# A rewritten work order for the first stage of a linear-attention and feed-forward kernel, with thirteen weight slices in place of ten beside the attention

## The chip, the core and the metric

The kernel runs on one core of one Trainium2 chip. A core has a matrix engine (PE, whose weight loads are shown apart as PEld), a vector engine (DVE), a scalar engine (ACT), a general engine (POOL) and a queue engine (SP) that only issues DMAs. Each engine works through its own instructions strictly in the order in which they were written, and waits at semaphores for what the others have to finish. The metric is the device time of one execution in microseconds (us); less is better.

## The reference, cut to what matters

```python
# q, k, v: (8 batches, 8 heads, 576 tokens, 64); omega: (128, 64)
q_s, k_s = q * scale, k * scale
def phi(x):
    proj = einsum('bhsd,md->bhsm', x, omega)
    h = proj - sum(x * x, axis=-1, keepdims=True) / 2
    h = h - max(h, axis=-1, keepdims=True)
    return exp(h) / sqrt(m)
q_p, k_p = phi(q_s), phi(k_s)
kv = einsum('bhsm,bhsd->bhmd', k_p, v)
z = sum(k_p, axis=2)
num = einsum('bhsm,bhmd->bhsd', q_p, kv)
den = einsum('bhsm,bhm->bhs', q_p, z)[..., None] + 1e-6
x = (num / den) as (4608 tokens, 512)
h = x @ w_in                      # (512, 2048), float64 weights
out = (h - tanh(h)) @ w_out       # (2048, 512), float64 weights
```

## The kernel before

**Tiling.** The 4608 tokens are cut into 18 chunks of 256. Eight heads are handled as four pairs (index c, 0 to 3). The 2048 hidden units are cut into 16 slices of 128 (index f, 0 to f in hexadecimal). A slice of the weights holds 128 columns of `w_in` and the matching 128 rows of `w_out`. The weights arrive as float64; the kernel decodes each slice to a high and a low part (two float32r numbers) and multiplies high by high, high by low and low by high.

**The first stage** does everything at once: the attention of batches 0 and 1 (unit `k<b><c>` for the keys, `q<chunk><c>` for the queries of chunks 0 to 2), the decoding of all 16 weight slices (`d<f>`), and the feed-forward of chunks 0 and 1 together (`f<s>`, 512 tokens wide). Its order is written out by hand, or by a program, in the string `ORDER`: each token names a unit, a step of it and, where needed, a buffer slot. `q12.pj.7` is the projection of chunk 1, pair 2, into PSUM bank 7. Lines 678 to 682 of the program walk through the tokens and emit each step's instructions, so the order of the tokens is the order of the instructions on every engine, SP and POOL included. No engine takes work out of this order.

**Steps of a key unit k.** `lk` and `lv` load keys and values (L474, L478, on SP), `pool` copies the last 64 keys and values of each head into the zeroed tiles `kd` and `vd` (L483, L484, four copies on POOL), `pjA`, `pjB`, `pj5` project (L454, L488, PE), `red*` take a row minimum (L460, L492, DVE), `exp*` the exponential (L465, L496, ACT), `pk0` and `pk1` sum keys by values (L500, L510, PE), `z`, `zt`, `zb` spread the key sums, `kvf`, `kvwa`, `kvwd` copy the result out.

**Steps of a query unit q.** `lq` loads (L550, SP), `pj`, `red`, `exp` as above, `den` the denominators (L561, DVE), `nD` and `nA` divide, `pt` transposes (L580, PE), `qt` copies (ACT), `pn` multiplies by the key-value sums (L590, PE), `xh` and `xl` split the result into high and low (L594, L604).

**Steps of a slice d.** `ld` loads 1 MB of float64 words (L618, SP), `b` scales the upper words (L623, ACT), `cl` clamps (L627: POOL, or DVE for slices 0 and 1), `v1`, `v2`, `v3` put the bits together (L630 to L637, DVE), `hi` writes the high part of the weights and `nh` its second copy (L642, L645, ACT), `di` is a DMA that POOL issues and that adds the decoded number to the second copy, so that the low part is left (L648). Only when this DMA has landed can the slice be used in full.

**Steps of a feed-forward unit f.** `h` is 12 matmuls of 512 columns (L380), of which the third already needs the slice's low part; `th`, `g`, `gh`, `gl` form h - tanh(h) and split it (ACT, DVE, ACT, DVE); `o` is 12 more matmuls (L410 to L412). `f0` to `fd` stand in the table; the last two slices follow it in `step`.

**Buffers.** `NW = 10` slices have a place of their own beside the attention's buffers (pool `a0`). The other six take the space of `a0`, which is closed at the token `da.ld`: `if f == NW: close_pool("a0")`, L614. SP therefore waits at these loads for the last users of the attention's buffers. Key, value and query loads rotate through three, three and two buffers.

After the table, the chunks 2 to 17 are processed in a steady loop with the feed-forward of a chunk beside the attention of later ones; there a scheduler, not the table, sets the order.

Of the kernel before, what the change touches and what calls it, by code (L numbers as in the profile page):

```python
# [33 lines left out]
ORDER = """
k03.lk.0 q00.lq.0 k00.lk.1 k02.lk.2 q02.lq.1 k03.lv.0 q00.pj.0 d1.ld q02.pj.1 q00.red k03.pjB.2 k03.pool
q00.exp.0 q02.red k00.pjB.3 k03.redB q02.exp.1 q12.lq.0 k03.pj5.4 k00.redB q03.lq.1 k03.pjA.5 k03.expB.2
k00.lv.1 k03.red5 k00.pjA.6 k03.redA k00.expB.3 k13.lk.0 q12.pj.7 k00.redA k03.expA.4 k02.lv.2 q03.pj.0 q12.red
k00.expA.5 k00.pool q01.lq.0 k03.pk0.3 q10.lq.1 q03.red d3.ld k03.exp5.0 k13.pjB.1 q03.exp.6 k02.pool k03.pk1
k13.redB q12.exp.7 q01.pj.2 k03.z k13.expB.2 k03.zt q01.red k11.lk.1 q10.pj.5 k03.kvf k03.zb d1.b.0 q03.den
k00.pj5.6 k13.lv.0 k00.pk0.4 q01.exp.4 q13.lq.0 k02.pj5.0 q10.red k13.pjA.7 d0.ld q03.nA q03.nD k02.red5  # L40
k02.pjA.1 d3.b.1 k13.redA k13.pool k00.red5 q03.pt.3 k02.redA k00.exp5.1 k02.pjB.2 q10.exp.6 d1.cl d3.cl
k00.pk1 d1.v1 q03.qt.0 k01.lk.0 k02.redB k02.exp5.0 q03.pn.6 k00.kvf k12.lv.1 d1.v2 k02.expB.3 k13.pj5.5
k11.pjA.3 k12.lk.2 k13.red5 k13.expA.5 k00.z d1.v3 k00.zt q20.lq.1 k01.pjB.0 k00.zb d4.ld d0.b.2 q00.den
k13.pk0.4 d1.hi k12.pool k12.pjB.2 q00.nD q10.den q00.nA k01.pjA.7 k13.exp5.1 q03.xh q00.pt.5 d1.nh d9.ld
k11.redA k13.pk1 q03.xl q10.nA q10.nD d1.di k01.redB k12.pj5.6 q00.qt.1 k13.kvwa k12.red5 k01.expB.0 k13.z
q00.pn.5 k01.redA d0.cl k13.zt q00.xh k01.lv.0 q10.pt.0 d0.v1 k13.zb k02.expA.2 q00.xl d6.ld k13.kvwd q20.pj.5
d3.v1 q10.qt.0 d3.v2 k13.kvf k12.exp5.1 q10.pn.1 k01.expA.5 k01.pool k02.pk0.4 q20.red q10.xh d4.b.0 d0.v2
k02.pk1 q11.lq.1 d2.ld q20.exp.6 q10.xl d4.cl k01.pj5.0 k02.z k12.pjA.6 d0.v3 k02.kvf k11.expA.2 k02.zt
k01.pk0.7 k12.redA k02.zb k01.red5 q11.pj.1 k12.expA.3 k12.redB q12.den k11.lv.2 q13.pj.5 k01.exp5.0 d0.hi
q22.lq.1 k01.pk1 q12.nD d7.ld q12.nA q02.den k11.pjB.3 d0.nh k11.pool q02.nD q12.pt.4 q02.nA q11.red q22.pj.6  # L50
k01.kvf k11.redB q12.qt.1 d0.di k11.pj5.0 q11.exp.0 q13.red q12.pn.4 k10.lv.0 k11.red5 q22.red k11.expB.5
q02.pt.1 k10.lk.0 d4.v1 q12.xh k01.z d4.v2 d5.ld q02.qt.0 k01.zt q13.exp.7 q02.pn.3 q12.xl d4.v3 k12.expB.1
k11.pk0.4 k10.pool k10.pjB.1 k01.zb q13.den d4.hi q23.lq.0 k10.pj5.5 k10.pjA.2 q21.lq.1 k11.exp5.0 q01.den
q13.nA d8.ld k11.pk1 q02.xh d2.b.2 q11.den q23.pj.7 k11.kvf k11.kvwa d2.cl q22.exp.2 q11.nD q21.pj.0 q13.nD
q02.xl q11.nA q01.nD q13.pt.6 q01.nA k11.z k11.kvwd q11.pt.3 k10.redA q13.qt.1 k11.zt k10.redB k11.zb q01.pt.6
q11.qt.0 k10.red5 q13.pn.4 q21.red k10.expB.5 q23.red q11.pn.3 q01.qt.1 d2.v1 q13.xh q01.pn.1 k10.expA.7 d2.v2
k12.pk0.6 q01.xh q13.xl q11.xh q01.xl d4.nh k12.pk1 q11.xl d2.v3 q23.exp.0 d4.di k10.pk0.4 k12.z d3.v3 k12.kvwa
k12.zt k12.kvf d2.hi f1.h.7 k12.kvwd q23.den k12.zb d3.hi d2.nh f0.h.6 q22.den f1.th d2.di q23.nA d7.b.0 f1.g
q22.nA q23.nD d7.cl f4.h.7 q22.nD f1.gh d3.nh f1.gl f0.th k10.exp5.0 f0.g q21.exp.4 q22.pt.2 f2.h.6 d6.b.2
q21.den d3.di f0.gh d6.cl q22.qt.0 f0.gl q21.nA q22.pn.1 q21.nD f4.th d7.v1 q23.pt.3 q22.xh f4.g k10.pk1  # L60
q23.qt.1 d7.v2 f0.o k10.kvwa k10.kvf d5.b.1 k10.z k10.kvwd d6.v1 d6.v2 d5.cl d6.v3 f1.o f4.gh f4.gl d6.hi d7.v3
f2.th d6.nh q23.pn.0 f2.g d5.v1 k10.zt f2.gh d6.di q21.pt.7 d5.v2 k10.zb f3.h.6 d7.hi f2.gl q23.xh d7.nh
q20.den q21.qt.0 d7.di f2.o f3.th q20.nD q20.nA f3.g d5.v3 d8.b.2 q20.pt.4 d5.hi d8.cl f6.h.7 q20.qt.1 f3.gh
d9.b.0 f3.gl d5.nh q20.pn.0 q21.pn.6 f6.th d5.di q20.xh d8.v1 f3.o q21.xh f6.g d9.cl da.ld d8.v2 d8.v3 f4.o
f6.gh d8.hi f6.gl db.ld d8.nh d9.v1 d9.v2 f5.h.6 d8.di da.b.1 d9.v3 da.cl dd.ld d9.hi f7.h.7 f5.th d9.nh f5.g
f5.gh dc.ld db.b.2 f5.gl d9.di f8.h.6 da.v1 f7.th db.cl da.v2 da.v3 f5.o de.ld f7.g da.hi da.nh db.v1 f6.o
dc.b.0 da.di db.v2 df.ld f7.gh dc.cl db.v3 f9.h.7 f7.gl db.hi db.nh f8.th db.di dd.b.1 f7.o f8.g dc.v1 f8.gh
dd.cl dc.v2 f8.gl fa.h.6 dc.v3 f9.th f9.g dc.hi f9.gh f8.o dd.v1 df.b.2 f9.gl dd.v2 fa.th df.cl dc.nh fa.g
fb.h.7 dd.v3 fa.gh fa.gl dd.hi dd.nh f9.o dc.di df.v1 fb.th df.v2 dd.di fb.g fa.o df.v3 fb.gh fb.gl df.hi
de.b.0 fc.h.6 df.nh de.cl fd.h.7 fc.th fc.g fc.gh df.di fc.gl fb.o de.v1 fd.th de.v2 fd.g de.v3 fc.o fd.gh  # L70
fd.gl de.hi de.nh fd.o de.di
# [4 lines left out]
def favor_attention_ffn(ctx: ExitStack, tc: tile.TileContext, qT, kT, va, vt, omT, w, out):  # L76
# [74 lines left out]
    nc.gpsimd.tensor_scalar(om_bd[D:P, 1], omf[D:P], -SCALE, 1.0, op0=ALU.mult, op1=ALU.mult)
# [4 lines left out]
    def kv_tiles(pool, names):

        ts = [(pool.tile([P, 9, E], F32, name=f"v{i}"), pool.tile([P, P], F32, name=f"kd{i}"),
               pool.tile([P, 2, E], F32, name=f"vd{i}")) for i in names]
# [4 lines left out]
        return ts

# [303 lines left out]
    def native_k(b, c):  # L469
        u, n = {}, f"k{b}{c}"  # L470

        def lk(slot):
            u["f"] = tile_at("kf", slot, [P, S], F32, f"{n}_f")
            nc.sync.dma_start(u["f"], kT[c, :, b * S : (b + 1) * S])  # L474

        def lv(slot):
            u["v"], u["kd"], u["vd"] = vtiles[slot]
            nc.sync.dma_start(u["v"][:, :, 0:D], va[b, c])  # L478

        def pool():  # L480
            for h in range(2):
                r = slice(h * D, h * D + D)
                nc.gpsimd.tensor_copy(u["kd"][r, r], u["f"][r, 4 * P : S])  # L483
                nc.gpsimd.tensor_copy(u["vd"][r, h], u["v"][r, 4])  # L484

        def pj5(slot):
            u["pj5"] = ps.tile([P, M], F32, tag=BANKS[slot], name=f"{n}_pj5")
            nc.tensor.matmul(u["pj5"], u["kd"], oms, start=True, stop=True)  # L488
# [9 lines left out]
        def pk(h):  # L498
            for t in range(4):
                nc.tensor.matmul(u["pk"][:, E * h : E * h + E], u["ph", 2 * (t // 2)][:, 2 * (t % 2) + h],  # L500
                                 u["v"][:, 5 * h + t], start=(h, t) == (0, 0), stop=False)
# [6 lines left out]
        def pk1():  # L508
            pk(1)
            nc.tensor.matmul(u["pk"][:, 0 : 2 * E], u["ph5"], u["vd"].rearrange("p h e -> p (h e)"),  # L510
                             start=False, stop=True)
# [21 lines left out]
        def zb():  # L533
            zb = att("zb0" if b == 0 else "zb", [P, 2, M], F32, f"{n}_zb")
            nc.scalar.copy(zb.rearrange("p h m -> p (h m)"), u["pk"][:, 256:512])
# [74 lines left out]
    def decoder(f):  # L610
# [9 lines left out]
        def b(slot):  # L620
            u["a"] = dec.tile([P, 2 * DM], U32, tag=f"a{slot}", name=f"a{f}")
            u["af"] = u["a"].bitcast(F32)
            nc.scalar.activation(u["af"], u["raw"].bitcast(F32)[:, 1::2], AF.Copy, scale=2.0**-112)  # L623

        def clamp():
            engine = nc.vector if f < 2 else nc.gpsimd
            engine.tensor_scalar(u["af"], u["af"], -TOP, TOP, op0=ALU.max, op1=ALU.min)  # L627

        def shift():
            nc.vector.tensor_scalar(u["a"], u["a"], 3, None, op0=ALU.logical_shift_left)  # L630

        def low():
# [151 lines left out]
```

## Time and profile before

| | us |
|---|---|
| median of 3 runs | 1075.91 |
| lowest and highest | 1070.32, 1076.04 |
| the profiled execution | 1073.08 |
| its span (first to last instruction) | 1071.3 |

The profiled execution lies 2.8 us under the median, inside the three runs. What lies outside the span is 1.8 us.

PE is busy for 97% of the span, DVE for 78%, ACT for 65%, POOL for 31%. These are averages over a first stage of about 170 us, in which all engines and the DMA queues are loaded, and a steady loop of about 900 us in which PE is hardly ever idle. In 40 slices of the span, the DMA engines' share (in tenths) begins with 8973842111: the first stage loads the attention's inputs and 16 MB of weights. Matmuls are pipelined, so the distance between the starts of two of them says more than the duration of one.

### The profile page before, as it was taken

What the parts mean: (1) busy time and instruction counts of PE and PEld (TensorE: products, weight loads), DVE (VectorE), ACT (ScalarE), POOL (GpSimd) and SP (SyncE); (2) the same over time, 40 slices, a digit from 0 to 9 for tenths busy, and PEclk for the clock granted to TensorE, in tenths of its full rate; (3) what the DMA queues carried; (4) which work ended last, traced back from release to release, by engine and by line L of the source; (5) the groups of instructions that cost most, each with busy time, mean ns of one, the idle gap of its engine ahead of it and who ended that gap; (6) DMA issues with size and microseconds to landing.
All of it is one profiled execution on the core that took longest, in us unless ns stands there. A gap on an engine that the chain in (4) does not pass through costs nothing.

```text
span 1071.3 us, 20143 instructions
## 1 busy us (share of the span) xinstructions
PE 1042.3 (97%) x6760; PEld 948.5 (89%) x6760; DVE 832.1 (78%) x2878; ACT 693.4 (65%) x1773; POOL 333.6 (31%) x569
## 2 busy tenths in 40 slices
...
GB/s 253 291 235 69 260 84 64 52 38 43 33 53 33 54 32 31 11 52 34 52 33 43 43 28 52 32 44 32 52 22 47 34 41 11 31 11 26 1 21 20
DMA packets 37831, 64.27 MB, mean 60 GB/s; under 512 B 12512, under 2 KB 21856, under 8 KB 35680
## 3 DMA queue, kind: packets, MB, share of 16 engines
...
q8 instruction: 53, 0.87, 0.3%
...
## 4 chain that ended last, share of the span: by engine, by line
PE 85%; DVE 6%; DMA 4%; ACT 3%; issue 1%; POOL 1%; SPq 0%; DVEq 0%; ACTq 0%; POOLq 0%
PE h L380 35%; PE po L410 11%; PE po L411 11%; PE po L412 11%; PE pk L243 3%; PE pj_q L184 2%; PE pt L332 2%; PE pn L344 2%; DMA w<-a 1%; PE pn L343 1%; DMA k_f<-kT 1%; PE k_pj L454 1%; PE pj_kb L184 1%; PE pj_ka L184 1%; PE k_pk L500 1%
## 5 line engine op out<-in xcount | busy, mean ns | idle before, releaser
L380 PE MATMUL h<-xh,w 128*128 128x256 f32 (+1 forms) x2176 | 451.3, 291 | 8.6 <-DMA w<-a 5.2
L380 PEld LDWEIGHTS h<-xh,w 128*128 128x128 f32 x2176 | 356.2, 191 | 19.6 <-DMA w<-a 5.9
L380 PE MATMUL h<-xl,w 128*128 128x256 f32 (+1 forms) x1088 | 317.1, 292 | 1.1 <-DVE xl L357 1.1
L380 PEld LDWEIGHTS h<-xl,w 128*128 128x128 f32 x1088 | 208.1, 191 | 7.5 <-DVE xl L357 1.3
L410 PE MATMUL po<-w,gh 128*128 128x512 f32 x544 | 213.9, 393 | 0.2 <-ACT gh L391 0.2
L411 PE MATMUL po<-w,gh 128*128 128x512 f32 x544 | 213.5, 392 | 0.0
L412 PE MATMUL po<-w,gl 128*128 128x512 f32 x544 | 211.5, 391 | 0.0
L391 ACT CAST gh<-g 128x512 fp32r<-128x512 f32 x144 | 89.5, 621 | 100.8 <-DVE g L388 94.4
L388 DVE TENSOR_TENSOR g<-h,g 128x512 f32<-128x512 f32 x144 | 98.8, 686 | 64.6 <-ACT g L386 63.4
L386 ACT ACTIVATE g<-h 128x512 f32<-128x512 f32 x144 | 85.2, 592 | 92.7 <-PE h L380 79.7
L394 DVE TENSOR_TENSOR gl<-g,gh 128x512 fp32r<-128x512 f32 x144 | 111.0, 771 | 41.0 <-ACT gh L391 39.2
L412 PEld LDWEIGHTS po<-w,gl 128*128 128x128 f32 x544 | 102.3, 188 | 20.9
L410 PEld LDWEIGHTS po<-w,gh 128*128 128x128 f32 x544 | 102.5, 188 | 16.7 <-ACT gh L391 0.4
L411 PEld LDWEIGHTS po<-w,gh 128*128 128x128 f32 x544 | 102.5, 188 | 15.3
L192 ACT ACTIVATE phi_q<-phi_q,nb_q 128x128 f32<-128x128 f32 x240 | 79.3, 392 | 5.8 <-DVE nb_q L188 5.5
L322 DVE CUSTOM_DVE_ANT_0 junk<-phi_q,zb 128x128 f32<-128x128 f32 (+1 forms) x240 | 71.8, 299 | 13.2 <-ACT phi_q L192 0.3
L235 POOL CAST vhl<-v 128x128 fp32r<-128x128 f32 (+1 forms) x144 | 46.1, 321 | 87.5 <-PE pk L243 74.5
L227 POOL TENSOR_TENSOR khl<-phi_ka,khl 128x256 fp32r<-128x256 f32 x48 | 37.5, 788 | 110.3 <-DVE khl L226 102.1
L337 DVE TENSOR_TENSOR ql<-pt,qh 128x512 fp32r<-128x512 f32 x60 | 41.1, 685 | 30.2 <-ACT qh L336 30.0
L627 POOL TENSOR_SCALAR a<-a 128x1024 f32<-128x1024 f32 x14 | 54.5, 3892 | 17.4 <-ACT a L623 17.0
L188 DVE CUSTOM_DVE_ANT_0 phi_q<-pj_q,phi_q 128x128 f32<-128x128 f32 x240 | 56.0, 284 | 1.3 <-ACT phi_q L185 1.0
L336 ACT CAST qh<-pt 128x512 fp32r<-128x512 f32 x60 | 34.9, 581 | 32.2 <-PE pt L332 32.0
...
## 6 DMA issues: line engine op xcount, KB each, us to landing
...
qf<-qT SPq DMA_DIRECT2D x60, 128.0 KB, 2.1
...
```

The lines of the kernel that those rows point to most:

```text
L188: nc.vector.tensor_tensor_reduce(ph[:, j], pj[:, i, :M], ph[:, j], scale=-SCALE, scalar=3.0e38, op0=ALU.add, op1=ALU.min, accum_out=nb[:, ...
L192: nc.scalar.activation(ph[:, j], ph[:, j], AF.Exp, bias=nb[:, j : j + 1], scale=-1.0)
L322: nc.vector.tensor_tensor_reduce(bank("junk")[r], ph[r, i], kvs[b, c][1][r, h], scale=1.0, scalar=EPS, op0=ALU.mult, op1=ALU.add, accum_ou ...
L380: nc.tensor.matmul(o, w_, x, start=i == 0, stop=i == len(prods) - 1)
L386: nc.scalar.activation(g, p, AF.Tanh)
L388: nc.vector.tensor_sub(g, p, g)
L391: nc.scalar.copy(gh, g)
L394: nc.vector.tensor_sub(gl, g, gh.bitcast(F32))
L410: nc.tensor.matmul(po[t], h, wt[f][:, 0, DM:], start=first, stop=False)
L411: nc.tensor.matmul(po[t], h, wt[f][:, 1, DM:], start=False, stop=False)
L412: nc.tensor.matmul(po[t], l, wt[f][:, 0, DM:], start=False, stop=last)
L627: engine.tensor_scalar(u["af"], u["af"], -TOP, TOP, op0=ALU.max, op1=ALU.min)
```

## The change

Three things change together.

1. **The table.** All of `ORDER` is replaced. The steps are the same, without `pool`. The order of units, loads, slices and banks differs nearly everywhere. Its first line before and now:

```
k03.lk.0 q00.lq.0 k00.lk.1 k02.lk.2 q02.lq.1 k03.lv.0 q00.pj.0 d1.ld q02.pj.1 q00.red k03.pjB.2 k03.pool
q10.lq.0 q00.lq.1 k02.lk.0 k01.lk.1 k02.lv.0 q10.pj.0 k02.pjA.1 q10.red q12.lq.0 q00.pj.2 k01.lv.1 q10.exp.0
```

2. **Thirteen slices beside the attention.** `NW` goes from 10 to 13, so that only the last three slices wait for the attention's buffers. Space comes from the reserve for the descriptors of POOL's DMAs, which is cut to 4096 bytes a partition.

3. **Zeros of the last keys from DRAM.** The host lays out a new array `kn`, in which the last 64 keys of each head stand in a block-diagonal tile of 128 by 128 with zeros beside them, and `va` gets a tenth block for the values in the same way. The POOL copies of `pool` and the tiles `kd` and `vd` go. Each key load grows from 576 to 640 columns, each value load from 9 to 10 blocks of 256 bytes a partition.

At the start, the scaled copies of omega (`om_bd`, `oms`) are made on DVE and not on POOL, and the rounded copy on ACT and not on DVE.

```diff
-NW = 10
+NW = 13
 ...
+    om_bd = a0.tile([P, 2, M], F32, name="om_bd")
+    nc.vector.memset(om_bd, 0.0)
+    nc.vector.tensor_scalar(om_bd[0:D, 0], omf[0:D], -SCALE, 1.0, op0=ALU.mult, op1=ALU.mult)
+    nc.vector.tensor_scalar(om_bd[D:P, 1], omf[D:P], -SCALE, 1.0, op0=ALU.mult, op1=ALU.mult)
 ...
-    nc.vector.tensor_copy(om[:, 0], omf)
+    nc.scalar.copy(om[:, 0], omf)
 ...
-    nc.gpsimd.memset(om_bd, 0.0)
-    nc.gpsimd.tensor_scalar(om_bd[0:D, 0], omf[0:D], -SCALE, 1.0, op0=ALU.mult, op1=ALU.mult)
 ...
-            u["f"] = tile_at("kf", slot, [P, S], F32, f"{n}_f")
-            nc.sync.dma_start(u["f"], kT[c, :, b * S : (b + 1) * S])
+            u["f"] = tile_at("kf", slot, [P, 5 * P], F32, f"{n}_f")
+            nc.sync.dma_start(u["f"], kn[b, c])
 ...
-        def pool():
-            for h in range(2):
-                r = slice(h * D, h * D + D)
-                nc.gpsimd.tensor_copy(u["kd"][r, r], u["f"][r, 4 * P : S])
-                nc.gpsimd.tensor_copy(u["vd"][r, h], u["v"][r, 4])
 ...
-            nc.tensor.matmul(u["pj5"], u["kd"], oms, start=True, stop=True)
+            nc.tensor.matmul(u["pj5"], u["f"][:, 4 * P :], oms, start=True, stop=True)
 ...
+    vtiles = [a0.tile([P, 10, E], F32, name=f"v{i}") for i in range(3)]
+    for v in vtiles:
+        nc.gpsimd.memset(v[:, :, D:], 1.0)
+        nc.gpsimd.memset(v[D:P, 4, D:], 0.0)
+        nc.gpsimd.memset(v[0:D, 5, D:], 0.0)
 ...
+    nc = bacc.Bacc("TRN2", target_bir_lowering=False, num_devices=1,
+                   dynamic_dma_scratch_size=4096)
```

The diff also adds a second way to decode a slice, chosen by a string `TYPES`; all 16 letters choose the old way, and the new steps `m`, `v4` and `w` don't occur in the table.

The order moves three places on which the prediction rests. The first is SP at the start of the program; `k` and `q` are keys and queries, `v` values, `raw` the words of a slice (a decimal number). Before:

```order
L139 DMA omf_86<-omT 64x128
L474 DMA k03_f_142<-kT 128x576
L550 DMA q00_f_144<-qT 128x256
L474 DMA k00_f_146<-kT 128x576
L474 DMA k02_f_148<-kT 128x576
L550 DMA q02_f_150<-qT 128x256
L478 DMA v0_122<-va 128x9x64
L618 DMA raw1_156<-w 128x1024
L550 DMA q12_f_187<-qT 128x256
L550 DMA q03_f_193<-qT 128x256
```

Now:

```order
L140 DMA omf_86<-omT 64x128
L533 DMA q10_f_136<-qT 128x256
L533 DMA q00_f_138<-qT 128x256
L462 DMA k02_f_140<-kn 128x640
L462 DMA k01_f_142<-kn 128x640
L466 DMA v0_122<-va 128x10x64
L533 DMA q12_f_153<-qT 128x256
L466 DMA v1_123<-va 128x10x64
L533 DMA q23_f_200<-qT 128x256
L466 DMA v2_124<-va 128x10x64
L533 DMA q01_f_219<-qT 128x256
L462 DMA k12_f_233<-kn 128x640
```

The first slice (`raw1`, 1 MB) stood eighth; now the first one stands thirteenth, behind two small query loads, three key loads and three value loads.

The second is the end of the slices' loads on SP. Before, from the last slice that has its own place:

```order
L618 DMA raw8_778<-w 128x1024
L618 DMA raw10_1264<-w 128x1024
L618 DMA raw11_1286<-w 128x1024
L618 DMA raw13_1309<-w 128x1024
L618 DMA raw12_1332<-w 128x1024
L618 DMA raw14_1370<-w 128x1024
L618 DMA raw15_1393<-w 128x1024
```

Now, from the last key load on:

```order
L462 DMA k10_f_820<-kn 128x640
L533 DMA q22_f_828<-qT 128x256
L601 DMA raw11_843<-w 128x1024
L601 DMA raw6_915<-w 128x1024
L601 DMA raw7_957<-w 128x1024
L601 DMA raw8_1059<-w 128x1024
L601 DMA raw10_1083<-w 128x1024
L601 DMA raw12_1143<-w 128x1024
L601 DMA raw13_1321<-w 128x1024
L601 DMA raw15_1349<-w 128x1024
L601 DMA raw14_1418<-w 128x1024
```

Six slices (10 to 15) stood behind the closing of the attention's pool, now three do (13, 15, 14). Six others (11, 6, 7, 8, 10, 12) now follow one another with nothing between them.

The third is POOL where the feed-forward begins: `a` is a slice being clamped, `w<-a` the adding DMA that ends its decoding. Before:

```order
L648 DMA w0_632<-a0_429 128x1024
L483 COPY kd0_123<-k10_f_709 64x64
L484 COPY vd0_124<-v0_122 64x66
L627 TENSOR_SCALAR a2_786<-a2_786 128x1024
L648 DMA w4_757<-a4_563 128x1024
L648 DMA w2_918<-a2_786 128x1024
L627 TENSOR_SCALAR a7_973<-a7_973 128x1024
L648 DMA w3_944<-a3_346 128x1024
```

Now:

```order
L654 DMA w2_550<-a2_438 128x1024
L654 DMA w3_609<-a3_495 128x1024
L620 TENSOR_SCALAR a4_771<-a4_771 128x1024
L620 TENSOR_SCALAR a5_798<-a5_798 128x1024
L654 DMA w1_801<-a1_730 128x1024
L654 DMA w5_935<-a5_798 128x1024
L620 TENSOR_SCALAR a9_953<-a9_953 128x1024
L654 DMA w4_982<-a4_771 128x1024
```

Slice 1, which the second feed-forward step needs, is now finished by a DMA that stands behind the clamps of slices 4 and 5; slices 0, 2 and 3 are finished well ahead of it. The feed-forward steps begin with f0, f1, f2, f3 (before: f1, f0, f4, f2).

More of the change, by code (lines that the diff above doesn't have):

```diff
@@ L38 @@
[L38 to L57, printed above, removed]
@@ new lines @@
+k01.expA.3 q23.lq.1 k02.pjB.7 k00.lv.2 q12.red k01.exp5.0 k01.expB.4 k02.pj5.0 k02.redB q01.lq.0 k01.pk0.1
+q12.exp.5 k02.red5 k12.lk.2 q23.pj.2 k02.exp5.1 k02.expB.6 k01.pk1 d0.ld q23.red q23.exp.7 k02.pk0.4 k01.z
+k02.pk1 k01.kvf k12.pjA.3 k02.z k12.lv.1 k02.kvf k02.zt k12.redA k12.pjB.5 k02.zb q12.den q02.lq.1 k12.expA.3
+k12.pj5.6 k01.zt k00.lk.1 q01.pj.0 k01.zb q12.nD q12.nA k12.red5 k12.redB q11.lq.0 q12.pt.7 k12.exp5.0 d0.b.0
+k03.lk.0 q01.red q02.pj.2 q12.qt.0 d0.cl d2.ld k12.expB.4 q12.pn.4 d0.v1 q02.red q01.exp.1 k12.pk0.3 q01.den
@@ new lines @@
+q20.pj.3 k00.expA.1 d2.v3 k11.pjB.1 k03.expB.6 q13.red d4.ld k00.pk0.2 k11.redB d2.hi k00.pk1 d3.v1 d2.nh
+q20.red k03.pk0.0 k00.z k03.red5 k11.expB.1 d3.v2 k00.zt d2.di k13.lk.1 k00.zb k11.pj5.1 d3.v3 k00.kvf
+k03.exp5.0 k03.pk1 q13.exp.5 q10.den k11.pjA.2 d3.hi q10.nD q10.nA q00.den k13.pjB.4 d3.nh k10.lv.2 q10.pt.5
+k11.redA q00.nA d3.di q00.nD q10.qt.1 d1.ld k03.z k11.red5 k11.expA.3 k03.zt k13.redB q10.pn.5 k11.exp5.1
+q00.pt.2 k03.zb q10.xh q03.den k11.pk0.1 q00.qt.0 k03.kvf q00.pn.2 q11.exp.6 q13.den k13.pj5.0 k11.pk1 q00.xh
@@ new lines @@
+q03.nA q11.den q13.nA k13.pjA.6 k11.kvwa k11.kvf q10.xl q11.nA q00.xl d5.ld k11.z d1.b.0 q13.nD k11.zt q03.nD
+q13.pt.5 q11.nD q03.pt.2 k11.zb k13.red5 q13.qt.1 k11.kvwd d1.cl q03.qt.0 q11.pt.1 k13.exp5.0 q13.pn.5 d1.v1
+d4.b.1 d1.v2 q03.pn.2 k13.lv.1 q13.xh q11.qt.1 d4.cl q13.xl q03.xh k13.redA q11.pn.0 k13.expB.0 d9.ld q03.xl
+d1.v3 d5.b.2 q11.xh d1.hi q11.xl f0.h.1 d5.cl d1.nh d4.v1 k10.lk.0 d4.v2 q21.exp.2 q22.lq.0 q21.den k13.expA.1
+db.ld k13.pk0.5 f0.th q20.exp.3 f0.g k10.pjA.2 d1.di d5.v1 q21.nA k13.pk1 q21.nD f0.gh d5.v2 k10.pj5.4 q21.pt.0
```

136 lines of the change are left out of this document (84 added, 52 removed).

## The prediction

> **What bounds the kernel now.** First the page's shares by engine, then the busy time in stretches that I cut along the first stage, last the list of what PE waited for.
>
> ```profile
> PE 1042.3 (97%) x6760; PEld 948.5 (89%) x6760; DVE 832.1 (78%) x2878; ACT 693.4 (65%) x1773; POOL 333.6 (31%) x569
> ```
>
> ```profile
> 10.00:60.00 50.00, 42.92 (x253) 37.21 (x253) 41.54 (x138) 45.66 (x143) 16.84 (x31) 0.98 0.92 287
> ...
> 70.00:110.00 40.00, 39.79 (x215) 33.99 (x214) 32.86 (x92) 33.15 (x67) 23.36 (x11) 1.00 0.40 78
> 110.00:120.00 10.00, 4.81 (x18) 3.61 (x17) 4.76 (x5) 4.05 (x5) 3.00 (x3) 0.87 1.02 315
> ...
> 170.00:190.00 20.00, 17.83 (x113) 15.99 (x112) 13.08 (x44) 12.23 (x29) 1.05 (x3) 1.00 0.19 62
> sum 190.00, PE 171.94 PEld 145.64 DVE 133.42 ACT 132.78 POOL 83.66; mean PE 21.49 PEld 18.20 DVE 16.68 ACT 16.60 POOL 10.46
> ```
>
> The columns are the stretch, its length, the busy time of PE, PEld, DVE, ACT and POOL, PE's granted clock, the DMA share and GB/s. PE is idle for 29.0 us of the span (1071.3 - 1042.3), and 18.1 us of that lie in these 190 us (190 less the 171.94 of the last row, which sums all stretches, those left out here too). So the change, which touches this stage alone, can win some 18 us and the slowed clock around the waits; the work of PE itself is the same before and after. In 10 to 60 us the DMA engines are busy 92% and ACT 45.66 of 50 us: these two, not PE, set the pace of the attention. From 70 us on PE is dense but for one hole at 110 to 120.
>
> ```profile
> PE k_pj L454 <- DMA k_f<-kT: 3.8, 2, 2.8
> PE k_pj L488 <- POOL kd L483: 1.5, 1, 1.5
> PE q_pj L454 <- DMA q_f<-qT: 1.4, 1, 1.4
> PE q_pj L454 <- POOL om_bd L151: 0.6, 1, 0.6
> ...
> PE h L380 <- DMA w<-a: 5.2, 1, 5.2
> PE h L380 <- DVE g L388: 2.4, 2, 2.2
> ```
>
> These are total, number and longest wait. Four of them are early loads and POOL copies (7.3 us), one is a slice's low part that came late (5.2), one lies behind the table (2.2, at 171 us).
>
> **A measure: PE's lag.** I count the PE work that the table puts ahead of a step and take it from the time at which that step starts. The lag is all that was lost up to there. The work is counted in distances between starts:
>
> ```profile
> 34.06 0.60 PE L580 MATMUL q_pt<-ident,q_phi 128*128 128x128 f32 x4
> 34.50 1.00 PE L500 MATMUL k_pk<-v,k_phi 128*128 128x66 f32 x8
> 35.34 0.44 PE L510 MATMUL k_pk<-vd,k_ph 128*128 128x132 f32 x2
> 35.62 0.38 PE L488 MATMUL k_pj<-oms,kd 128*128 128x128 f32 x2
> 35.84 1.03 PE L590 MATMUL q_pn<-q_qt,kvf 128*128 128x256 f32 x4
> 36.71 0.38 PE L530 MATMUL k_pk<-ident,k_z 128*128 128x128 f32 x2
> ...
> 44.52 1.03 PE L454 MATMUL k_pj<-om_bd,k_f 128*128 128x256 f32 x4
> 45.39 0.38 PE L530 MATMUL k_pk<-ident,k_z 128*128 128x128 f32 x2
> ...
> 73.81 0.48 PE L380 MATMUL h<-xh,w 128*128 128x512 f32 x1
> ```
>
> A `pt` takes 0.44 us, `pk0` 0.84 (counted 0.86), `pk1` 1.12 (0.84 and 0.28), `pj5` 0.22, `pn` 0.87, a projection 0.87; `zt` I count as 0.22. Before, ahead of the first feed-forward step f1 stand 28 projections, 8 `pj5`, 8 `pk0`, 7 `pk1`, 7 `zt`, 8 `pt` and 8 `pn`: 52.9 us. It starts at 73.81, so the lag is 20.9 us. The next rows show the hole and what follows:
>
> ```profile
> 112.42 0.39 PE L380 MATMUL h<-xl,w 128*128 128x512 f32 x1
> 117.99 1.22 PE L380 MATMUL h<-xh,w 128*128 128x512 f32 x2 [5.19 <-DMA w<-a]
> ...
> 121.24 0.40 PE L380 MATMUL h<-xl,w 128*128 128x512 f32 x1
> ...
> 148.93 0.39 PE L410 MATMUL po<-w,gh 128*128 128x512 f32 x1
> 151.65 0.39 PE L380 MATMUL h<-xh,w 128*128 128x512 f32 x1
> 157.22 0.39 PE L410 MATMUL po<-w,gh 128*128 128x512 f32 x1
> ```
>
> From 148.93 to 151.65 runs one `o`, to 157.22 two `h`: about 2.73 us each. Step f5 starts at 112.19 (one matmul of 0.23 before the first row) with 90.4 us of work ahead, a lag of 21.8. Step fc starts at 151.65 with 123.1 ahead, a lag of 28.5. The growth of 6.8 us is the hole: the third matmul would have come at 112.65 and came at 117.99 (5.3 us), and the eight matmuls from there to 121.24 took 3.25 us where 8 x 0.227 is 1.8 (1.4 us, while the stretch from 110 shows a clock of 0.87).
>
> [...]
>
> **The change, part by part.**
>
> *Start and loads.* The first projection waits no more for POOL's `om_bd`: DVE makes it in three small instructions. Its first loads are 0.26 MB of queries, and the second projection needs 0.59 MB in all (two queries of 128 KB, a key of 320) where it needed 1.15 (three keys of 288, two queries). So the waits of 0.6 and 1.4 us go or shrink to a few tenths. The last key load k10 had 14.4 MB in front of it, its own included (10 queries, 8 keys, 8 values, 8 slices), and the 40.8 us of PE work ahead of its use; now it has 14.0 MB (11, 8, 8 and 7) and 50.6 us. So the 3.8 us for keys go. Counted inside those 14.0 MB are 32 KB more in each of 16 key and value loads: 0.5 MB, at 287 GB/s 1.8 us of DMA time in the stretch that the DMAs fill. They are hidden while a load is early, which the 10 us of PE work now cover; uncovered they cost at most 1.8 us.
>
> *The POOL copies.* 32 copies go, and with them the wait of 1.5 us. The scaling that DVE takes over stands before its first reduction; bounds are 0 and the 0.6 us that PE waited for it on POOL. I take 0. The smaller descriptor reserve has no row: 0, or a wait for the DMA before, at most one landing of 4.6 us; nearest are two adding DMAs issued 0.9 us apart, so I take 0 and keep the end in the range.
>
> *What is late next: ACT.* With the loads early, ACT sets the pace.
>
> ```profile
> 7.36 1.14 ACT L465 ACTIVATE q_phi<-q_pj,q_nb 128x128 f32<-128x128 f32 x4 [4.43 <-DVE q_nb L460]
> ...
> 20.68 0.33 ACT L526 COPY kvf<-k_pk 128x64 f32<-128x64 f32 x2 [0.49 <-issue]
> 20.89 0.39 ACT L535 COPY k_zb<-k_pk 128x256 f32<-128x256 f32 x1
> 21.15 1.18 ACT L623 ACTIVATE a<-raw 128x1024 f32<-128x1024 f32 x1
> 22.20 1.16 ACT L465 ACTIVATE q_phi<-q_pj,q_nb 128x128 f32<-128x128 f32 x4
> 23.20 0.74 ACT L573 ACTIVATE q_phi<-q_phi,q_dn 128x128 f32<-128x128 f32 x2
> 23.79 1.18 ACT L623 ACTIVATE a<-raw 128x1024 f32<-128x1024 f32 x1
> ...
> 26.09 0.64 ACT L584 COPY q_qt<-q_pt 128x512 f32<-128x512 f32 x1
> ...
> 30.67 1.03 ACT L642 CAST w<-a 128x1024 fp32r<-128x1024 f32 x1
> ...
> 32.45 0.35 ACT L594 CAST xh<-q_pn 128x256 fp32r<-128x256 f32 x1
> ```
>
> By starts, `kvf` takes 0.21 us, `zb` 0.26, `b` 1.05, four exponentials 1.0, `nA` 0.59: each 0.1 to 0.15 less than its duration. By the same discount `qt` is 0.5, `hi` and `nh` 0.93, `xh` 0.25. Ahead of f1 the new table puts on ACT 27 groups of four exponentials (27), 8 single ones (2), 6 `b` (6.3), 9 `hi` or `nh` (8.4), 9 `nA` (5.3), 9 `qt` (4.5), 9 `xh` (2.3), 6 `zb` (1.6), 7 `kvf` (1.5) and 5 others (1.5): 60.4 us. ACT's first exponential starts some 1 us earlier, at 6.3, for the 0.6 us of `om_bd` and the earlier query. Idle between, as in the stretch of 10 to 60 us (4.3 of 50), are 5.2. So f1 is due at 6.3 + 60.4 + 5.2 = 71.9 us, or about 71.5, as the last of these steps are not f1's own. PE work ahead of it is 56.3 us (the sum above with one `h` of 2.73, one `pn` of 1.1 and one `pt` more and one `pk0` less): a lag of 15.2 in place of 20.9.
>
> *A new wait at f1.* Its slice 1 is finished by an adding DMA behind two clamps on POOL (the third place shown of the order). ACT's part for slice 1 is done when 52 us of ACT's work are, at 6.3 + 52 + 4.5 = 63; clamps of slices 4 and 5 on POOL end near 65. The landing times of the adding DMAs, minimum, median and maximum, for those issued in 30 to 55, 70 to 100 and 105 to 115 us:
>
> ```profile
> DMA to landing us min/median/max: 7.2/7.7/8.3
> ...
> DMA to landing us min/median/max: 4.5/4.6/5.0
> ...
> DMA to landing us min/median/max: 9.8/10.5/11.2
> ```
>
> Early and at the hole, raw loads fill the queues; in between it is quiet. At 65 us six slices follow one another on SP, so the DMAs are full: 65 + 8 = 73 us, 1.3 us after f1's third matmul is due (71.5 + 0.45). Bounds: 0 (4.6 us) and 4.3 (11.2). I take 1.3: lag 16.5, a gain of 4.4 so far. Behind that wait PE's f2 and f3 stand, whose slices are ready, and ACT waits for f1's sums.
>
> *The hole.* Only three slices, not six, wait for the attention's buffers; the row is that of the landing maximum 11.2 beside this burst. Slice 10 is now the one finished within it, with 8.3 us of PE work between its adding DMA and its use, where slice 5 had 5.5. A landing of 9.8 to 11.2 leaves a wait of 1.0 to 2.4; 4.6 leaves none. I take 0.8, where 6.8 were lost: a gain of 6.0.
>
> *Behind the table* the 2.2 us stay.
>
> **Sum** against the profiled execution: 1073.1 - 4.4 - 6.0 = 1062.7, said as 1063. That execution lies 2.8 us under the median; against it the same gain reads 1065.5.
>
> **The rivals.**
>
> *ACT and its chains give the early gain back* (0.18): for it, ACT is already busy 91% in 10 to 60 us; against it, some of its idle time was due to keys that came late. Then only the hole goes: 1073.1 - 6.0 = 1067.
>
> *The order does not do what it says* (0.12): waits reappear one for one elsewhere, as k10's load lies near its use. 1073.
>
> *The adding DMAs fall behind: slower* (0.10). Nothing holds SP between the six loads of slices 11 to 12, so they go out together. PE work between adding DMA and use is 4.9 us for slice 1, 5.7, 5.9 and 6.6 for 6, 7 and 8, 8.3 for 10 and 8.2 for 13; 0.45 us more each until the third matmul. At a landing of 9.8 us the waits are 4.4, 3.6, 3.4, 2.7, 1.0 and 1.1, in all 16.2, and 1.4 for the clock on the first three: 20.4. Gained are 5.7 at f1 and 6.8 at the hole: 1073.1 + 7.9 = 1081. It decides from a landing of about 8.8 us on (the same sums give 12.5 there), if that lasts until slice 8 is finished, near 105 us. Against it: attention and 13 slices are 20 MB, 70 us at 287 GB/s, so with the adding DMAs between them the loads end by about 90.
>
> [...]
>
> **How the numbers follow.** My forecast, 1063 (1055 to 1068), has 0.60, the rivals 0.18, 0.12 and 0.10. The range 1055 to 1074 holds all but the slower rival and some tails; its low end is a first stage in which also the wait at f1 and half of ACT's idle time vanish (1.3 + 0.8 + 2.6 + 2.2 behind the table: about 1056). Faster or slower means by over 0.5%, about what a measurement of this kernel can tell from no change. Faster: 0.60 and two thirds of 0.18, 0.72; same: the rest of it and 0.12, 0.18; slower: 0.10.
>
> **What would show it.** Right: the first `h` (f0) near 61 us and f1 near 71.5; no wait of PE for `k_f` or POOL; a wait of 0 to 4 us for `w<-a` at f1; nothing over 2.5 us at 110 to 130; fc's lag 17 to 19. Wrong: PE waiting for `w<-a` several times, landings over 8.8 us beyond 90 us, or ACT idle more than 10 us before f1.

## The result and the profile after

| | before | after |
|---|---|---|
| median, us (11 runs each) | 1073.02 | 1066.22 |
| lowest and highest | 1070.32, 1076.04 | 1064.18, 1068.78 |
| profiled execution | 1073.08 | 1067.96 |
| its span | 1071.3 | 1066.1 |

The ratio of the runs is 0.9938, with a 95% interval of 0.9921 to 0.9955: 6.8 us or 0.62% faster, where 10.4 us were forecast. The time, 1066, lies in the predicted range, 3 us above the predicted 1063.

First come the shares of the profile of the changed kernel, then its stretches (length, busy time of PE, PEld, DVE, ACT, POOL, granted clock, DMA share, GB/s).

```profile
PE 1042.6 (98%) x6760; PEld 946.6 (89%) x6760; DVE 831.3 (78%) x2881; ACT 693.8 (65%) x1774; POOL 321.3 (30%) x533
```

```profile
0.00:10.00 10.00, 8.08 (x33) 6.92 (x34) 3.50 (x9) 3.73 (x10) 3.51 (x23) 1.00 0.66 176
10.00:60.00 50.00, 44.98 (x280) 39.09 (x278) 42.51 (x145) 47.02 (x148) 12.14 (x6) 1.00 0.93 263
...
70.00:110.00 40.00, 36.43 (x179) 30.51 (x178) 30.19 (x77) 28.93 (x54) 20.01 (x10) 0.96 0.60 156
110.00:120.00 10.00, 10.00 (x50) 8.44 (x49) 7.37 (x8) 6.59 (x9) 8.22 (x3) 1.00 0.38 83
...
sum 190.00, PE 175.93 PEld 148.32 DVE 137.51 ACT 136.69 POOL 77.11; mean PE 21.99 PEld 18.54 DVE 17.19 ACT 17.09 POOL 9.64
```

The hole at 110 to 120 us is closed (PE 10.00 of 10, before 4.81). In 10 to 60 us PE has 2.1 us more of its work done (44.98 against 42.92). But 70 to 110, dense before (39.79 of 40), now has 3.6 us idle and a clock of 0.96. PE's waits of the first 190 us (total, number, longest) name the place:

```profile
PE h L368 <- DMA w<-a: 3.6, 1, 3.6
PE q_pj L442 <- DMA q_f<-qT: 1.5, 1, 1.5
PE k_pk L513 <- DVE k_z L497: 1.4, 1, 1.4
PE h L368 <- DVE g L376: 1.2, 1, 1.2
...
PE k_pj L442 <- DMA k_f<-kn: 0.9, 1, 0.9
...
PE po L398 <- ACT gh L379: 0.8, 1, 0.8
```

The timeline of PE at that place is f1, with fc behind it:

```profile
60.68 0.58 PE L368 MATMUL h<-xh,w 128*128 128x512 f32 x1
...
72.91 0.58 PE L368 MATMUL h<-xh,w 128*128 128x512 f32 x1
73.33 0.40 PE L368 MATMUL h<-xl,w 128*128 128x512 f32 x1
77.30 0.74 PE L368 MATMUL h<-xh,w 128*128 128x512 f32 x2 [3.57 <-DMA w<-a]
...
78.99 1.05 PE L368 MATMUL h<-xh,w 128*128 128x512 f32 x2
79.84 0.63 PE L368 MATMUL h<-xl,w 128*128 128x512 f32 x1
...
146.80 0.39 PE L368 MATMUL h<-xh,w 128*128 128x512 f32 x1
```

f0 starts at 60.68 and f1 at 72.91. The third matmul of f1 waits 3.57 us for slice 1's adding DMA, and soon after it pairs of matmuls take 1.05 us where they take 0.62 elsewhere: the clock fell (0.82 in 76 to 80 us, 0.75 in 80 to 84). What happened to POOL shows when that DMA was issued: two clamps (slices 4 and 5) run from 59.20, and the issue comes behind them.

```profile
59.20 7.60 POOL L620 TENSOR_SCALAR a<-a 128x1024 f32<-128x1024 f32 x2 [9.69 <-ACT a L609]
66.76 0.90 POOL L654 DMA_DIRECT2D w<-a  x1
```

It landed at 77.25, 10.5 us later. The lags, by the count of the prediction (start less PE work ahead), with a second profiled execution of the same kernel (run after_again, below):

| | before | predicted | after | after_again |
|---|---|---|---|---|
| start of f1 | 73.81 | 71.5 | 72.91 | 72.31 |
| lag there | 20.9 | 15.2 | 16.6 | 16.0 |
| wait at f1 | none | 1.3 | 3.57 | 3.17 |
| lag behind it (f4; before: f5) | 21.8 | 16.5 | 22.3 | 19.7 |
| lag at fc | 28.5 | 17 to 19 | 23.7 | 21.5 |
| wait behind the table | 2.2 | 2.2 | 1.2 | 1.2 |

Ahead of f4 stand 74.9 us of work, and it starts at 97.20 and 94.56. In the profiled execution the wait at f1 took back the whole early gain, and what is left by fc is the hole's.

### The profile page after: what moved, and what is told of

Its sections match the earlier page's. It is cut to its first block, busy times and chain, and to the rows that moved or that the text cites. A ratio compares the mean times of both kernels' runs of the same rounds, so it can differ in the third digit from the quotient of the medians.

```text
span 1066.1 us, 20100 instructions
## 1 busy us (share of the span) xinstructions
PE 1042.6 (98%) x6760; PEld 946.6 (89%) x6760; DVE 831.3 (78%) x2881; ACT 693.8 (65%) x1774; POOL 321.3 (30%) x533
## 4 chain that ended last, share of the span: by engine, by line
PE 78%; DVE 11%; issue 4%; DMA 3%; ACT 2%; POOL 2%; SPq 0%; DVEq 0%; POOLq 0%; ACTq 0%
PE h L368 33%; PE po L398 10%; PE po L399 10%; PE po L400 10%; PE pk L231 2%; PE pj_q L172 2%; DMA w<-a 2%; PE pt L320 2%; PE pn L332 1%; PE pn L331 1%; DVE a L640 1%; POOL a L620 1%; DVE junk L310 1%; DVE a L632 1%; PE pj_kb L172 1%
## 5 line engine op out<-in xcount | busy, mean ns | idle before, releaser
L382 DVE TENSOR_TENSOR gl<-g,gh 128x512 fp32r<-128x512 f32 x144 | 108.7, 755 | 43.9 <-ACT gh L379 42.0
L400 PEld LDWEIGHTS po<-w,gl 128*128 128x128 f32 x544 | 102.2, 188 | 21.8 <-DVE gl L382 0.9
L399 PEld LDWEIGHTS po<-w,gh 128*128 128x128 f32 x544 | 102.6, 189 | 15.2
L223 POOL CAST vhl<-v 128x128 fp32r<-128x128 f32 (+1 forms) x144 | 44.5, 310 | 88.6 <-PE pk L231 74.9
## 6 DMA issues: line engine op xcount, KB each, us to landing
raw<-w SPq DMA_DIRECT2D x16, 1024.0 KB, 10.4
```

The costliest lines, as they stand in the source:

```text
L382: nc.vector.tensor_sub(gl, g, gh.bitcast(F32))
L399: nc.tensor.matmul(po[t], h, wt[f][:, 1, DM:], start=False, stop=False)
L400: nc.tensor.matmul(po[t], l, wt[f][:, 0, DM:], start=False, stop=last)
```

## The experiments

Every time is a median, and its ratio is to the kernel before on the same chip: 1074.64 us in the first four runs, 1073.78 in the next four, 1074.28 in the last three. The first four ran on one chip, the other seven on another, so times of the two groups are compared by what they gain over the kernel before.

### Use slice 1 later

All steps of f1 and f3 change names; the two places of their matmuls:

```diff
-q22.exp.4 q22.den d5.hi f1.h.3 d5.nh k10.redB
+q22.exp.4 q22.den d5.hi f3.h.3 d5.nh k10.redB
...
-k10.expB.6 f2.h.0 d9.cl f0.gl d4.hi d4.nh f1.th f3.h.4
+k10.expB.6 f2.h.0 d9.cl f0.gl d4.hi d4.nh f3.th f1.h.4
```

> Table of the changed kernel with the feed-forward units f1 and f3 exchanged (f0, f3, f2, f1), nothing else. Between the two places lie 5.4 us of PE work. Theory (the missing gain is the wait of 3.9 us and the slowed clock of 1.4 us at f1, because slice 1's adding DMA lands at 77.25 us): slice 1's low part is now due at 78.4 + 0.45, so no PE wait for an adding DMA; the lag at fc falls from 23.7 to 18 to 19; 1061 to 1062 us, against 1066.2 for the changed kernel. Rival (ACT's chain sets the pace there anyway and the wait only covers it): PE waits at the same place for ACT or DVE instead, lag at fc stays 22 to 24; 1065 to 1066. Rival (the wait moves on to the next slices, whose adding DMAs land 8 us after issue): a wait of 2 to 4 us at f4 or f5; 1065.

Measured (run swap13): 1064.24 us, ratio 0.9907 (0.9888 to 0.9926). The wait for the DMA is gone and the clock stays at 1.00 from 70 to 110 us, so the cover decided that wait. But fc starts at 144.66, a lag of 21.6, no better than the 21.5 of after_again. PE's timeline shows new waits where the old one had stood in front of them:

```profile
81.53 0.62 PE L563 MATMUL q_pt<-ident,q_phi 128*128 128x128 f32 x2 [0.62 <-ACT q_phi L556]
...
83.94 0.75 PE L563 MATMUL q_pt<-ident,q_phi 128*128 128x128 f32 x4 [0.95 <-DVE q_phi L551]
...
130.66 0.50 PE L398 MATMUL po<-w,gh 128*128 128x512 f32 x1 [2.08 <-ACT gh L379]
```

The first two are the divisions of the last queries, the third a copy on ACT that stands behind the decoding of slice c. The times of the theory (1061 to 1062) and its lag (18 to 19) were missed. The first rival is half right: just behind the wait, ACT and DVE are no earlier than PE needs them.

### Take the raw loads out of the burst

```diff
-nc.sync.dma_start(u["raw"], w[f])
+(nc.scalar if f in (6, 7, 8, 10, 11, 12) else nc.sync).dma_start(u["raw"], w[f])
```

> The six slice loads that SP issued back to back from 56 to 62 us (slices 6, 7, 8, a, b, c) are issued from ACT's queue at their places in the table; nothing else. Theory (the adding DMA of slice 1 lands late because it stands among 6 MB of raw words): ACT's own work spreads the loads over 60 to 85 us, the adding DMA of slice 1 lands 5 to 8 us after its issue in place of 10.5, the wait at f1 falls from 3.6 to 0 to 1.5 us; 1062 to 1064, with up to 2.4 us of ACT time for six issues of 0.4 us against it. Rival (POOL's late issue is the whole of it; the landing does not depend on what else is queued): landing stays 9.5 to 11, wait 3 to 4; 1066 to 1068.

Measured (run gate): 1063.99 us, ratio 0.9913 (0.9893 to 0.9932). Below are DMA queues (q1: SP's loads, q0: POOL's adding DMAs; packets, MB, share of 16 engines) and issues (KB, time to landing): of the changed kernel in four pieces of 2 us from 66 to 74 us, then of this run in 64 to 70.

```profile
q1 hardware_dynamic: 117, 0.83, 99.4%
...
w<-a POOLq DMA_DIRECT2D x1, 512.0 KB, 10.5
...
q1 hardware_dynamic: 113, 0.85, 102.2%
...
q1 hardware_dynamic: 74, 0.55, 69.2%
q0 software_dynamic: 29, 0.12, 30.2%
...
q0 software_dynamic: 56, 0.23, 57.2%
q1 hardware_dynamic: 53, 0.38, 47.1%
```

```profile
raw<-w ACTq DMA_DIRECT2D x1, 1024.0 KB, 4.7
w<-a POOLq DMA_DIRECT2D x1, 512.0 KB, 5.1
```

In the changed kernel the DMA issued at 66.76 moves no packet before 70.8 us, and then shares the engines about evenly with the loads. In gate, issued at 68.66, it moves its first packet at 70.1, and it lands in 5.1 us; the wait at f1 is gone. So the raw loads make the landing late, partly before its first packet (4.1 us after the issue in place of 1.4), partly after it (6.4 us in place of 3.7). The edit spreads the loads in time and also moves them to another queue; which of the two helped was not tried apart. In the profiled execution fc's lag was still 24.6, as this execution lost 2.7 us at 38 us (the changed kernel 1.5) to a late query load, with a slowed clock behind it (0.75 in 36 to 40 us, 0.82 in 40 to 44); that is ahead of all that the edit changes.

### Issue slice 1's adding DMA earlier

```diff
-q11.xl f0.h.1 d5.cl d1.nh d4.v1
+q11.xl f0.h.1 d1.nh d4.v1
...
-k10.pjA.2 d1.di d5.v1 q21.nA
+k10.pjA.2 d1.di d5.cl d5.v1 q21.nA
```

> On POOL the adding DMA of slice 1 goes ahead of the clamp of slice 5 (one token moved behind another); nothing else. Theory (issue order on POOL is half of the wait): issue at 64.4 us, when ACT has finished slice 1, in place of 66.8; landing 10 us later at 74.5 to 75, the wait at f1 falls from 3.6 to 1 to 1.5 us, too short to slow the clock; 1062.5 to 1064. The clamp of slice 5 ends 2 us later, and DVE waits for it: up to 2 us against it. Rival (the queues are emptied in order, so the adding DMA lands when the raw words ahead of it are through, at about 77, whenever it is issued): no change, 1066.

Measured (run di_first): 1063.99 us, ratio 0.9907 (0.9889 to 0.9924).

```profile
63.71 0.90 POOL L654 DMA_DIRECT2D w<-a  x1 [1.45 <-ACT q_phi L453]
```

```profile
74.42 0.72 PE L368 MATMUL h<-xh,w 128*128 128x512 f32 x2 [0.81 <-DMA w<-a]
```

Issued 3 us earlier, it lands 2.9 us earlier (74.38) after nearly the same time, 10.7 us, and the wait is 0.81. So the landing is not a fixed moment at which the queues run dry; the place behind the clamps is worth 2.8 us of wait (2.4 against after_again). The lag at fc is 20.9.

### Relieve ACT

For slices 0, 2 and 3, step b:

```diff
-nc.scalar.activation(u["af"], topf, AF.Copy, scale=2.0**-112)
+nc.gpsimd.tensor_scalar(u["af"], topf, 2.0**-112, 1.0, op0=ALU.mult, op1=ALU.mult)
```

> The scaling of slices 0, 2 and 3 (step b, 1.05 us each on ACT) is done by POOL, which is busy for 12 of the 50 us from 10 to 60; nothing else. Theory (ACT, busy 47.0 of these 50 us, sets the pace of the attention, not the DMAs at 93%): f0 starts 2 to 3 us earlier than 60.7, at 57.7 to 58.7, and the adding DMA of slice 1 is issued as much earlier, so that the wait at f1 stays and the whole gains 2 to 3 us: 1063 to 1064. Rival (the loads set the pace): f0 at 60 to 61, no change, 1066.

Measured (run b_pool): 1066.99 us, ratio 0.9930 (0.9915 to 0.9945), no gain over the changed kernel.

```profile
10.00:60.00 50.00, 45.31 (x278) 38.57 (x276) 43.46 (x143) 44.60 (x143) 15.96 (x9) 1.00 0.94 272
```

```profile
72.08 0.58 PE L368 MATMUL h<-xh,w 128*128 128x512 f32 x1
72.50 0.40 PE L368 MATMUL h<-xl,w 128*128 128x512 f32 x1
76.27 1.06 PE L368 MATMUL h<-xh,w 128*128 128x512 f32 x2 [3.37 <-DMA w<-a]
```

ACT has 2.4 us less to do in 10 to 60 us (44.60 against 47.02), and f1 starts at 72.08, 0.2 us before that of after_again. The expectation fell: ACT's work did not set the pace of the attention. f0 starts at 59.87, where the rival (the loads set the pace) had 60 to 61; that agrees with the rival and does not prove it.

### One part of the change at a time

Third part alone: table of before without `pool`, ten slices.

```diff
-NW = 13
+NW = 10
```

> The table of the kernel before (without the pool steps), ten slices and the default descriptor reserve, with the third part of the change alone: zeros of the last keys and values from DRAM, the scaled omega on DVE. Theory (this part is worth only its own waits, and 0.5 MB of zeros is hidden): the waits of 1.5 us for POOL's kd and 0.6 for om_bd go and come back in part as waits for keys; 0 to 2 us under the kernel before, the hole at 112 us stays. Rival (POOL's copies were what made the early stage late): f1 starts 4 to 6 us earlier than 73.8 and the whole gains 4 us.

Measured (run zeros): 1073.74 us, ratio 0.9997 (0.9980 to 1.0013). No gain by itself is measured: the waits for POOL are gone (2.1 us before), but PE waits 9.0 us for keys and queries where it waited 5.2. The hole stays:

```profile
119.41 0.80 PE L368 MATMUL h<-xh,w 128*128 128x512 f32 x1 [5.60 <-DMA w<-a]
```

Then thirteen slices beside the same table:

```diff
-da.ld db.ld dd.ld dc.ld
+da.ld db.ld dc.ld dd.ld
-NW = 10
+NW = 13
```

> As the run before it (table of before, zeros from DRAM), with thirteen slices beside the attention and the descriptor reserve of 4096 bytes; the load of slice c goes ahead of that of slice d, so that only d, e and f wait for the attention's buffers. Theory (not the number of loads in the late burst but the cover that the order gives decided): with a, b and c loaded early the burst is one slice and the loads of the next chunk; the adding DMA of slice 5 lands still 7 us or more after issue, the wait at f5 shrinks from 5.2 to 1 to 3 us and f8, whose slice follows with 2.8 us of cover, waits in its place: 0 to 2.5 us gained over the run before it. Rival (my prediction's reason: fewer slices waiting removes the hole): landing 4.6 to 6 us, no wait over 1 us between 105 and 130 us, 5 to 7 us gained.

Measured (run nw13): 1071.91 us, ratio 0.9973 (0.9959 to 0.9988), 1.8 us under the run before it by the medians.

```profile
120.46 0.80 PE L368 MATMUL h<-xh,w 128*128 128x512 f32 x1 [4.33 <-DMA w<-a]
```

With three raw loads in the burst in place of four (of the six that stood behind the closing, two had gone out at 54 to 57 us), the adding DMA takes 10.4 us in place of 11.6, and the wait is 4.33 against 5.60, more than the 1 to 3 expected. So the fourth load is worth 1.2 us of landing, not the hole. By the medians some 2 us of the change are due to the number of slices, though the two intervals overlap. The rest is put down to the order by subtraction; the new order with ten slices was not run.

### Only exchange f5 and f7 in the kernel before

All their steps change names; of their matmuls:

```diff
-f5.h
+f7.h
...
-f7.h
+f5.h
```

> The kernel before with the feed-forward units f5 and f7 exchanged, nothing else: slice 5 is then used 2.7 us of PE work later. Theory (the hole is a shortage of cover for two late landings, slice 5's at 117.95 and slice 8's at 123.3 us): two waits of 2 to 3 us at f5 and f8 in place of one of 5.2, too short to slow the clock; 0 to 2 us gained. Rival (slice 5 alone is late): one wait of 2.5 us, 3 to 4 us gained.

Measured (run b_swap57): 1073.96 us, ratio 1.0002 (0.9987 to 1.0018).

```profile
118.05 0.73 PE L379 MATMUL h<-xh,w 128*128 128x512 f32 x2 [2.33 <-DMA w<-a]
...
121.41 0.50 PE L379 MATMUL h<-xh,w 128*128 128x512 f32 x1 [0.80 <-DVE g L387]
...
123.38 1.06 PE L379 MATMUL h<-xh,w 128*128 128x512 f32 x2 [1.23 <-DMA w<-a]
```

```profile
124.00:128.00 4.00, 4.00 (x13) 3.14 (x12) 3.45 (x3) 2.14 (x4) 3.33 (x1) 0.62 1.05 342
```

The hole is not one late slice: moved, it splits, and behind it slice 8's DMA is late too. That short waits don't slow the clock was my estimate, and the run shows otherwise: behind three of them, 4.4 us within 8, it stood at 0.62. The three cost as much as the one: from this place to fc the lag grows by 6.7 us, where it grew by 6.8.

### Repair the chains too

Beside the edits of swap13 and di_first:

```diff
-d4.hi d4.nh f1.th f3.h.4 k13.zb f1.g q22.nA q23.den
+k13.zb q22.nA d4.hi d4.nh f3.th f1.h.4 q23.den f3.g
-dc.v2 dc.v3 dc.hi f7.o f8.gh dc.nh f8.gl
+dc.v2 f8.gh f8.gl dc.v3 dc.hi f7.o dc.nh
```

> The changed kernel with four edits of its table: f1 and f3 exchanged; the adding DMA of slice 1 ahead of the clamp of slice 5 on POOL; the denominators of q23 ahead of f3's subtraction on DVE, with k13's key sums and q22's division ahead of slice 4's copies on ACT; f8's copy gh ahead of slice c's hi on ACT. Theory (what swap13 gained at f1 was given back in two ACT and DVE chains, 1.6 us near 82 and 1.3 us more at 130.7): no wait of PE over 0.5 us between 72 and 95 us, none over 1 us near 130, lag at fc 16.5 to 18; 1059 to 1061 us, 3 us under swap13. Rival (each repaired wait uncovers the next): lag at fc 20 or more, 1063 to 1064.

Measured (run combo): 1063.03 us, ratio 0.9898 (0.9875 to 0.9921). The lag at fc is 19.5, between the two expectations; the time is the rival's (1063 to 1064). The waits of 0.62 and 0.95 us are gone; one of 0.86 for a division at 69.8 came in, which stands on DVE behind the first step of slice 5, whose clamp is later now (di_first has it too, 0.87); and now slice a's adding DMA, issued at 123.60 and landed at 131.60 beside the late loads, is waited for:

```profile
131.65 0.73 PE L368 MATMUL h<-xh,w 128*128 128x512 f32 x2 [0.78 <-DMA w<-a]
```

The changed kernel and combo once more (after_again, combo_again), and then two more edits (combo2):

> The changed kernel itself, as the yardstick of the two runs beside it on the same chip. All theories: 1064 to 1068 us, ratio to the kernel before 0.993 to 0.995, a wait of 3 to 4 us for slice 1's adding DMA at f1.

> The kernel of the run combo once more, beside the changed kernel. Theory (its gain of 3 us over the changed kernel is real): 1062 to 1064 us, ratio to the changed kernel 0.996 to 0.998. Rival (a difference between chips): same as the changed kernel within 1 us.

```diff
-d1.di d5.cl d5.v1 q21.nA k13.pk1 q21.nD f0.gh
+d1.di d5.cl q21.nA k13.pk1 q21.nD d5.v1 f0.gh
...
-da.v3 dc.cl f7.gl
+da.v3 f7.gl
...
-f8.g da.di dc.v1 f6.o dc.v2 f8.gh f8.gl dc.v3
+f8.g da.di dc.cl f8.gh f8.gl dc.v1 f6.o dc.v2 dc.v3
```

> The kernel of combo with two more edits of the table: the adding DMA of slice a ahead of the clamp of slice c on POOL, with f8's copies ahead of slice c's steps on DVE; and q21's division ahead of slice 5's first step on DVE. Theory (the waits left in combo are 0.86 us at 69.8 for q21's division and 0.78 us at 131.65 for slice a's adding DMA, each with nothing late behind it): both go, slice a's adding DMA is issued 1 us earlier and lands near 130.5; 1.0 to 1.6 us under combo. Rival (slice c and slice 5 come later and are waited for in their place): within 0.5 us of combo.

| | us | ratio to before | lag at fc |
|---|---|---|---|
| after_again | 1065.62 | 0.9920 (0.9903 to 0.9936) | 21.5 |
| combo_again | 1063.62 | 0.9901 (0.9882 to 0.9921) | 19.5 (combo) |
| combo2 | 1065.98 | 0.9923 (0.9905 to 0.9941) | 21.9 |

The combined version lies 2.0 us under the changed kernel on the same chip; the intervals overlap, so it is likely, not certain, that it beats it. It beats the kernel before by 10.7 us. That swap13, gate and di_first alone beat theirs by 10.4, 10.7 and 10.7 us is as much, so these runs do not show that the further repairs are worth anything. combo2 was a miss: the wait for slice a falls from 0.78 to 0.32 us, but slice c comes late in its place, as its rival said; its time is 2.4 us over combo_again, which is worse than the rival's 0.5:

```profile
135.50 0.50 PE L398 MATMUL po<-w,gh 128*128 128x512 f32 x1 [1.70 <-ACT gh L379]
```

## Why the prediction was right, and where not

**The number.** 1066 lies in the range, but the gain is 6.8 us and not 10.4. That the other reading, 1065.5 against the median of three runs, comes within 0.7 us is luck: the median of eleven runs of the kernel before lies 2.9 us lower.

**Start and loads: right in the main.** The waits for k10's load and for POOL are gone. Small load waits stayed (0.9 at 7 us, 1.5 at 37 us). The third part shows no gain by itself in the run zeros; with the new order its loads come early enough.

**ACT's pace: number near, reason wrong.** f1 was due at 71.5 and came at 72.91 and 72.31. The sum of ACT's work and its idle time gave nearly that, but the run b_pool took 2.4 us from ACT in that stretch and f1 hardly moved. PE was held by several small waits there (the query load, `k_z` on DVE, `kvw`, `xh` on ACT); which of them is the root was not tried.

**The wait at f1: right mechanism, wrong size. This is the term that failed.** The prediction said "I take 1.3", with bounds of 0 and 4.3, and the two traces show 3.57 and 3.17. Two of its inputs were off: the issue came at 66.76 and 66.15 in place of 65, and the landing took 10.5 and 10.1 us in place of 8. The landing of 8 us came from a row of only two DMAs (7.2 and 8.3); beside six raw loads the nearer row was the one at the old hole, 9.8 to 11.2, which I kept for the bound. The early row did not carry over either: in the changed kernel the DMAs of slices 0, 2 and 3, issued at 35 to 49 us, landed in 8.2 to 11.2, and only their long cover hid it. The runs gate and di_first show each input by itself. And the clock: I put no surcharge, and the profiled execution paid 1.5 us in f1 (from its start to f2's, less its work and the wait: 80.70 - 72.91 - 2.73 - 3.57) and 0.65 more in f2, 2.1 in all. The second one, whose clock stayed at 1.00, paid 0.5 by the same sum (78.72 - 72.31 - 2.73 - 3.17) and nothing in f2, so some 1.6 us are the clock's. I had both new waits under 2 us, and one of 2.2 us, at 171 us in the kernel before, had left the clock at 1.00; that no shorter one slows it was my estimate from this one wait. The wait came out longer, and I had overlooked that the kernel before has one of 2.78 us with a slower clock behind it:

```profile
59.09 1.75 PE L454 MATMUL k_pj<-om_bd,k_f 128*128 128x256 f32 x4 [2.78 <-DMA k_f<-kT]
```

```profile
60.00:70.00 10.00, 9.68 (x50) 7.94 (x50) 6.40 (x15) 5.89 (x22) 3.71 (x2) 0.86 0.90 350
```

These four matmuls take 1.75 us; four like them take 1.03 at 44.52.

**What the wait was worth.** From f1 to f4 the lag grows by 5.7 and 3.7 us. The run swap13 took the wait away, yet its lag at fc is only 2.1 us under the one profiled execution and level with the other. By the medians it gains 10.4 us over the kernel before, where the changed kernel gains 6.8 and 8.7: 1.7 to 3.6 more, with intervals that overlap. So part of the wait came back. ACT's and DVE's chains for the last queries stand right behind it and then hold PE. The rival "ACT and its chains give the early gain back", 1067, thus came close in time; in the profiled execution the early gain was given back, yet to the DMA first and to the chains only once that was repaired.

**The hole: right in size, half right in reason.** 6.0 us were to come back; PE waited there 0.8 us, and the lag grew by 1.4 from f4 to fc. That I had also put down 0.8 is luck: mine was for slice a's DMA, and this one, at 132.76, is for a copy on ACT (`gh`). My reason was the number of slices that wait for the attention's buffers. nw13 gives it some 2 us; the landing falls only to 10.4. The rest, by subtraction, is the order: slices a and b, not 5 and 8, are finished in the burst, and they have more cover. For slice a I had reckoned 8.3 us of cover and a wait of 1.0 to 2.4, or none, and taken 0.8, which neither bound gives. In the changed kernel its DMA landed at 135.75, and its matmul came at 136.38: no wait, because PE was late from f1. Where PE is 4 us earlier, in combo, the wait is 0.78.

**Behind the table: missed.** 2.2 us were to stay; 1.2 are left. All runs with the old table show 2.1 or 2.2 and all with the new one 1.18, so it belongs to the order.

**The rival that adding DMAs fall behind: right at slice 1 alone.** Behind slice 1, a landing over 8.8 us came again only in the late burst: slice b's, issued at 121.65, took 10.5. I had named that a sign of being wrong; no wait followed, as slice b is first used by fb, at 141.36. Those issued from 82 to 114.1 us took 4.5 to 5.0, so slices 6, 7 and 8 were in time. The turning point was not exact either: at a landing of 8.8 us the same sums give 11.9 to 14.7, by how many of the waits pay for the clock, and not 12.5, so it lies at 8.3 to 8.9. No run shows the term of this sum that charges the clock, 1.4 us each, to just the first three waits: a wait of 3.17 us left the clock at 1.00 (after_again), and behind one of 2.78 it stood at 0.65 (before, 60 to 64 us).

**The sum.** Lag 4.8 us less at fc and 1.0 behind the table are 5.8; the profiled pair differs by 5.1, and the 0.7 us between them, in the steady loop, I did not follow. The medians differ by 6.8, since the profiled execution is one of the longer ones of the changed kernel.
